# FFT and mixture of experts on one core: batch 2 transformed ahead of the first expert slot, scale products tied

## The chip, the cores and the metric

One core of a Trainium2 chip. The metric is the device time of one execution in microseconds (us); less is better. The engines are TensorE (PE; its weight loads are PEld), VectorE (DVE), ScalarE (ACT), GpSimd (POOL) and SyncE (SP), which here only issues DMAs.

## The reference

```python
X = np.fft.fft(x, axis=1)          # x: 8 x 2496 x 256
x = np.fft.fft(X, axis=2).real.reshape(19968, 256)
logits = x @ w_gate                # 8 experts
e_idx = np.argmax(logits, axis=1)
...
for e in range(8):
    mask = e_idx == e
    h = np.maximum(x[mask] @ w1[e], 0.0)     # 256 -> 1024
    ye = h @ w2[e]                           # 1024 -> 256
    out[mask] = gate_w[mask, None] * eom[mask, e, None] * ye
```

Each batch of 2496 rows goes through a two-dimensional Fourier transform, of which the real part is kept; each row then goes to the one expert that its gate picks, and the result is scaled by two gate values.

## The kernel before, in words

**Transform.** A batch comes as five column chunks (`xt`, 512 KB each). Each chunk is folded: `fold1` adds its halves (line 419), `fold2` makes sums and differences (`ft`, lines 437 to 452), and its squares are summed for a scale. `dstage` multiplies a chunk with a table (fp32 matmuls, line 492) into PSUM (`psb_t`, three buffers), and `devac` splits the result into two fp16 parts, `ahi` by ScalarE and `alo` by VectorE (lines 504, 505). `sstage(b, i)`, for i from 0 to 4, does the second transform in fp16 (line 556), and `sevac` makes rows of it (`eo`, `rt`, `rows`; lines 575 to 594). `gatepass` (line 537) computes the gates of batches 0 and 1 first; for the others the gate columns ride in `sstage`. `gating` finds expert, position and scale of each row (`desti`, `car`).

**Scatter.** `send` writes the rows into a scratch tensor `scr` in DRAM, sorted by expert: 20 indirect DMAs of 128 rows per batch, on GpSimd (line 705). Four DMAs of SP write zero rows at the end of the same tensor (line 1055).

**Experts.** Work is cut into slots of up to 256 rows. Round 0 has 16 slots (8 experts x 512 rows) and takes rows of batches 0 and 1 only, rounds 1 and 2 take rows of the batches up to 3 and up to 5, and a last part the rest. A slot loads its rows as `xr` (a transposing DMA) and their scale words `xf` (lines 1198, 1199); SP issues both. `mm1` computes `hp` (line 1266), `hh` and `hl` are its two fp16 parts (lines 1270, 1271), and `mm2` computes `yp` (line 1288). `ysc` is the product of the row's scale and the expert's (line 1292, VectorE, 128x2 elements), `y` the scaled result (line 1295), and GpSimd scatters it to the output. Weights of an expert are loaded in fp32 (`load_w`, line 1208), squared for a scale (`wenergy`, 1221; `wscale`), and split into two fp16 parts (`conv`, lines 1242 and 1243).

**Order.** `start` is written out by hand for all engines. In the second part, up to the first slots, only SP and GpSimd follow the written order (`PH1`); the order on TensorE, VectorE and ScalarE is set at build time by a scheduler, which works with its own estimates of when a DMA lands. VectorE's and ScalarE's queues are in order: an instruction that waits holds up all behind it. `steps` yields a step for each `sstage`: steps 0 to 9 are batches 0 and 1, 10 to 14 batch 2. `WEND` is the step after which the first slots' code is begun, `FSTART` the one after which slots and further steps alternate; PSUM is divided anew there (`hp` gets two buffers, `yp` one). `behind(eng)` has an instruction placed after the newest `hh` or `hl` of the slots, and `pin` keeps folds in the written order.

```python
MARGIN0 = 1
FSTART = 5 * BA + MARGIN0     # BA = 2
WEND = FSTART - 2
```

## Time and profile before

| | |
|---|---|
| median of 3 runs | 1108.4 us (1107.82 to 1110.0) |
| the profiled execution | 1108.73 us |
| its span, first to last instruction | 1107.0 us |
| TensorE busy | 1042.2 us (94%) |
| VectorE busy | 672.9 us (61%) |
| ScalarE busy | 598.9 us (54%) |
| GpSimd busy | 428.2 us (39%) |
| mean granted clock of TensorE | 0.979 |
| first slot's first matmul | 125.34 us |

All times in rows are from the start of the span. "Idle before" names what released an engine after it stood still. A busy share is a mean over stages with different limits, so it is to be read by stage. The granted clock is a share of full speed.

### The profile page before, as it was taken

How to read it: one execution, taken by the hardware profiler on the slowest of the kernel's cores; microseconds unless marked ns; L12 is line 12 of the kernel's file. 1: busy time of each engine (PE TensorE's matmuls, PEld its weight loads, DVE VectorE, ACT ScalarE, POOL GpSimd, SP SyncE). 2: the span in 40 equal slices, each digit the busy share in tenths (PEclk: the TensorE clock that was granted, in tenths of full speed). 3: DMA queues.
4: the chain of work that ended last, by engine and by line, in shares of the span. 5: the costliest groups of instructions: out<-in, count | busy, mean ns of one | idle time of the engine just before them, and what ended most of it. 6: DMA issues, size and time to landing. Idle time of an engine off the chain costs nothing. (4 is left out here: it accounts for less than half of the span.)

```text
span 1107.0 us, 27910 instructions
## 1 busy us (share of the span) xinstructions
PE 1042.2 (94%) x10226; PEld 934.3 (84%) x10226; DVE 672.9 (61%) x1351; ACT 598.9 (54%) x1099; POOL 428.2 (39%) x389
## 2 busy tenths in 40 slices
PE   5795598999998999999999999999999999999998
PEld 4584587888887999999998888888998979998997
DVE  5875558869689468557559554554355553555542
ACT  3366376667677456556554554544445553555542
POOL 0267114566478363436255771221221222212122
PEclk9897799999999999999999999999999999999999
DMA  9525373665577436556465896646556565575640
GB/s 367 182 77 189 118 186 102 166 188 183 132 175 201 101 111 156 132 154 168 130 174 121 205 198 165 158 96 180 137 134 189 143 173 130 149 165 159 156 102 28
DMA packets 152312, 171.02 MB, mean 154 GB/s; under 512 B 115309, under 2 KB 116207, under 8 KB 152164
## 3 DMA queue, kind: packets, MB, share of 16 engines
q1 hardware_dynamic: 136292, 126.48, 44.5%
q0 software_dynamic: 15728, 42.14, 11.7%
q8 instruction: 82, 1.34, 0.5%
q10 hardware_dynamic: 144, 0.52, 0.2%
q14 instruction: 66, 0.54, 0.2%
HBM read 149.51 MB, written 43.63 MB: 174 GB/s over the span
## 5 line engine op out<-in xcount | busy, mean ns | idle before, releaser
L1266 PE MATMUL hp<-xr,w0b 128*128 128x256 f16 (+2 forms) x4080 | 477.2, 267 | 11.3 <-DVE hl L1271 11.2
L1288 PE MATMUL yp<-w1b,hh 128*128 128x256 f16 x2560 | 438.5, 273 | 0.8 <-ACT y L1295 0.8
L1266 PEld LDWEIGHTS <-w0b 128*128 128x128 f16 x4080 | 380.8, 98 | 56.6 <-issue 10.4
L1296 POOL DMA_INDIRECT out_dram<-y,xf x160 | 188.7, 1179 | 549.7 <-ACT y L1295 501.0
L1288 PE MATMUL yp<-w1b,hl 128*128 128x256 f16 x1280 | 349.2, 273 | 0.0
L1271 DVE SCALAR_TENSOR_TENSOR hl<-hp,hh 128x512 f16<-128x512 f32 (+2 forms) x340 | 221.0, 654 | 204.0 <-ACT hh L1270 179.4
L1270 ACT ACTIVATE hh<-hp 128x512 f16<-128x512 f32 (+2 forms) x340 | 191.8, 567 | 247.0 <-PE hp L1266 244.7
L1288 PEld LDWEIGHTS <-hh 128*128 128x128 f16 x2560 | 248.1, 98 | 28.6 <-issue 1.3
L705 POOL DMA_INDIRECT scr<-rows,desti x160 | 173.0, 1081 | 59.2 <-issue 42.4
L1288 PEld LDWEIGHTS <-hl 128*128 128x128 f16 x1280 | 125.8, 98 | 14.6
L1295 ACT ACTIVATE y<-yp,ysc 128x256 f32<-128x256 f32 (+1 forms) x160 | 67.5, 470 | 43.7 <-PE yp L1288 39.2
L1243 DVE SCALAR_TENSOR_TENSOR w0b<-raw0b,wsc,w0b 128x1024 f16<-128x1024 f32 x44 | 58.3, 1325 | 48.5 <-ACT w0b L1242 48.5
L1243 DVE SCALAR_TENSOR_TENSOR w1b<-raw1b,wsc,w1b 128x1024 f16<-128x1024 f32 x44 | 56.4, 1283 | 39.6 <-ACT w1b L1242 37.9
L492 PE MATMUL psb_t<-tdet,ft 128*125 128x290 f32 (+1 forms) x200 | 60.7, 457 | 14.0 <-DVE alo L505 4.7
L1242 ACT ACTIVATE w0b<-raw0b,wsc 128x1024 f16<-128x1024 f32 x44 | 50.3, 1146 | 32.9 <-PE hp L1266 31.5
L492 PEld LDWEIGHTS psb_t<-tdet,ft 128*125 128x125 f32 (+1 forms) x200 | 40.5, 212 | 28.9 <-issue 12.9
L1242 ACT ACTIVATE w1b<-raw1b,wsc 128x1024 f16<-128x1024 f32 x44 | 50.4, 1147 | 14.4 <-PE yp L1288 13.2
L419 POOL TENSOR_TENSOR xt<-xt 128x500 f32<-128x500 f32 (+1 forms) x25 | 32.5, 1308 | 63.1 <-DMA xt<-in_xl_dram 28.8
L1243 DVE SCALAR_TENSOR_TENSOR w1b<-raw1b,ssc,w1b 128x1024 f16<-128x1024 f32 x32 | 41.0, 1282 | 23.7 <-ACT w1b L1242 22.8
L1243 DVE SCALAR_TENSOR_TENSOR w0b<-raw0b,ssc,w0b 128x1024 f16<-128x1024 f32 x32 | 40.8, 1282 | 22.0 <-ACT w0b L1242 21.5
L1242 ACT ACTIVATE w0b<-raw0b,ssc 128x1024 f16<-128x1024 f32 x32 | 36.4, 1145 | 14.3 <-DMA raw0b<-in_w_dram 13.2
L505 DVE SCALAR_TENSOR_TENSOR alo<-psb_t,p_x,ahi 125x580 f16<-125x580 f32 (+1 forms) x40 | 32.0, 816 | 19.1 <-ACT ahi L504 19.0
(221 smaller groups left out, 1008.4 us busy)
## 6 DMA issues: line engine op xcount, KB each, us to landing
raw0b<-in_w_dram SPq DMA_DIRECT2D x118, 512.0 KB
raw1b<-in_w_dram SPq DMA_DIRECT2D x118, 512.0 KB
xt<-in_xl_dram SPq DMA_DIRECT2D x40, 512.0 KB
scr<-rows,desti POOLq DMA_INDIRECT x160
out_dram<-y,xf POOLq DMA_INDIRECT x160
xr<-scr SPq DMA_TRANSPOSE x85
xf<-scr SPq DMA_DIRECT2D x75, 2.0 KB
tst<-in_ts_dram SPq DMA_DIRECT2D x2, 512.0 KB
```

The lines of the kernel that those rows point to most:

```text
L419: i = eng.tensor_tensor(x0, x0, x1, op=ALU.add)
L492: nc.tensor.matmul(o[:, 0:290], ft[:, k, par, W], tdab[:, k], start=(k == 0), stop=(k == 1))
L505: nc.vector.scalar_tensor_tensor(s["alo"][W, c], ps[W, :, 0:290], sc, s["ahi"][W, c], op0=ALU.mult, op1=ALU.subtract)
L705: free_order("scr", batch=b, inst=nc.gpsimd.indirect_dma_start(out=scr[:, :], out_offset=bass.IndirectOffsetOnAxis(ap=s["desti"][:, j:j + ...
L1242: nc.scalar.activation(w[:, 0], r, AF.Copy, scale=sc)
L1243: nc.vector.scalar_tensor_tensor(w[:, 1], r, sc, w[:, 0], op0=ALU.mult, op1=ALU.subtract)
L1266: nc.tensor.matmul(ps[:, k, T], w1v[:, hl, kc, (f % 4) * 128:(f % 4 + 1) * 128], a["x"][:, x, T], start=(m == 0), stop=(m == 5))
L1270: i = nc.scalar.activation(hh[:, G, T], ps[:, :, T], AF.Relu)
L1271: j = nc.vector.scalar_tensor_tensor(hl[:, G, T], ps[:, :, T], 0.0, hh[:, G, T], op0=ALU.max, op1=ALU.subtract)
L1288: nc.tensor.matmul(a["yp"][0:M, u], a[k, h][:, f, u * 128:u * 128 + M], w2v[:, hl, f], start=(g == 0 and f == 0 and m == 0), stop=(h == 1 ...
L1295: nc.scalar.activation(a["y"][0:M, u], a["yp"][0:M, u], AF.Copy, scale=ys[0:M, u:u + 1])
L1296: put = nc.gpsimd.indirect_dma_start(out=out[:, :], out_offset=bass.IndirectOffsetOnAxis(ap=a["f"].bitcast(I32)[0:M, u, 1:2], axis=0), in_ ...
```

## The change

Its parts:

- `FSTART` goes from 11 to 14 and `WEND` from 9 to 10, so all of batch 2's five steps are emitted before slots and steps alternate. Loads of the first slots and of the next weights, and `load_x`, now come at step 10; the second expert's four weight loads follow the first two `xr` and `xf` together.
- The four DMAs of zero rows move from behind the first weight loads into `start`, behind the loads of the tables.
- Batch 2's five `fold1` go from GpSimd to VectorE, and its folds are handed out in pieces behind the first gating and in steps 0 to 2 (`foldall`, `some`). Batch 3's folds may start at step 5 as before, but now all through `folds`.
- The second `gatepass` comes at step 2 instead of 1. The first expert's weights are squared at steps 1 and 2 instead of 6, scaled at step 4 instead of 8, and converted at steps 8 and 9 (w1) and 10 (w2).
- `ysc` is placed behind the newest `hl` (`behind("DVE")`) in rounds 0 to 2; before the last part the notes of the newest instructions are cleared.

```diff
--- before.py
+++ after.py
@@ -61,10 +61,10 @@
 SPL = (4, 9, 14)
 MARGIN = 2 + len(SPL)
 
-MARGIN0 = 1
+MARGIN0 = 4
 FSTART = 5 * BA + MARGIN0
 
-WEND = FSTART - 2
+WEND = 5 * BA
 
 AHEAD = (5, 6, 7, 8, 9)
 
@@ -376,7 +376,7 @@
         gens = []
         hold = []
 
-        newest, pinned = {}, []
+        newest, pinned, final = {}, [], []
 
         def behind(eng):
             return tc.issue_after(newest[eng]) if eng in newest else nullcontext()
@@ -983,6 +983,8 @@
                 load_t(j)
             fold(4)
             nc.sync.dma_start(tidt, tid)
+            for k in range(4):
+                nc.sync.dma_start(scr[DUM + 128 * k:DUM + 128 * (k + 1), :], ztile)
             scale(0)
             smalls.clear()
             for c in range(KC):
@@ -1002,7 +1004,7 @@
                 m = fq[0]
                 fq[0] += 1
                 dve = m // KC <= BA + 1
-                if m < NB * KC and m // KC != BA:
+                if m < NB * KC:
                     fold1(*divmod(m, KC), nc.vector if dve else nc.gpsimd)
                 while fq[1] < NB * KC and fq[1] <= m - (0 if fq[1] // KC <= BA + 1 else FLAG):
                     f = fold2(*divmod(fq[1], KC))
@@ -1023,6 +1025,18 @@
                 else:
                     p = None
 
+        def foldall(b):
+            for c in range(KC):
+                fold1(b, c, nc.vector)
+                yield
+                for _ in fold2(b, c):
+                    yield
+                yield
+
+        def some(g, k):
+            for _ in range(k):
+                next(g, None)
+
         def dparts(b):
             for c in range(KC):
                 dstage(b, c)
@@ -1040,8 +1054,6 @@
             folds(0, 2 * KC - 1)
             xcap[0] = NB * KC
             load_x()
-            for c in range(KC):
-                fold1(BA, c, nc.gpsimd)
             gatepass(0)
             add_gen(gating(0))
             for _ in sstage(0, 0):
@@ -1051,11 +1063,11 @@
             for m in range(2):
                 for h in range(2):
                     load_w(0, m, h)
-            for k in range(4):
-                nc.sync.dma_start(scr[DUM + 128 * k:DUM + 128 * (k + 1), :], ztile)
             weave(piece("A"))
+            fa = foldall(BA)
             weave(piece("C"), dparts(1))
             weave(piece("C"))
+            some(fa, 12)
             for n in range(5 * BA):
                 b, i = divmod(n, 5)
                 if n:
@@ -1064,22 +1076,23 @@
                     for _ in sevac(b, i):
                         pass
                 send(b, i)
-                if n == 1:
+                some(fa, 3 if n < 2 else 99)
+                if n == 2:
+                    fq[:] = 2 * [KC * (BA + 1)]
                     gatepass(1)
                     add_gen(gating(1))
-                ahead((0, 0, 12, 12, 99)[min(n, 4)])
+                ahead((0, 0, 8, 12, 99)[min(n, 4)])
                 if n == 4:
                     for _ in table_a(0):
                         pass
-                if n >= 5:
-                    folds(n, KC * BA + i, [])
-                if n == 6:
-                    for m in range(2):
-                        for h in range(2):
-                            wenergy(0, m, h)
-                if n == 8:
+                if n in (1, 2):
+                    for h in range(2):
+                        wenergy(0, n - 1, h)
+                if n == 4:
                     for m in range(2):
                         wscale(sched[0][1], m)
+                if n > 7:
+                    conv(0, 0, n - 8)
                 yield ("step", n)
             for n in range(5 * BA, 5 * NB):
                 b, i = divmod(n, 5)
@@ -1106,6 +1119,9 @@
                 next(sv)
                 for _ in sv:
                     pass
+                if n == 5 * BA:
+                    for h in range(2):
+                        conv(0, 1, h)
                 if i == 1 + (b == BA) and b + 1 < NB:
                     energy(b + 1)
                     energy_sum(b + 1)
@@ -1242,7 +1258,7 @@
                 nc.scalar.activation(w[:, 0], r, AF.Copy, scale=sc)
                 nc.vector.scalar_tensor_tensor(w[:, 1], r, sc, w[:, 0], op0=ALU.mult, op1=ALU.subtract)
             nxt = (after_new if wb == 0 else after_sing).get(n, NS)
-            if n or m:
+            if n:
                 chained(load_w, nxt, m, h)
             else:
                 late.append((nxt, m, h))
@@ -1269,7 +1285,7 @@
             hh, hl = a["hh", g // 2], a["hl", g // 2]
             i = nc.scalar.activation(hh[:, G, T], ps[:, :, T], AF.Relu)
             j = nc.vector.scalar_tensor_tensor(hl[:, G, T], ps[:, :, T], 0.0, hh[:, G, T], op0=ALU.max, op1=ALU.subtract)
-            if sched[n][0] < LAST:
+            if sched[n][0] < LAST and not final:
                 newest.update(ACT=getattr(i, "ins", i), DVE=getattr(j, "ins", j))
 
         def mm2(n, g):
@@ -1289,7 +1305,8 @@
                                      start=(g == 0 and f == 0 and m == 0), stop=(h == 1 and f == 3 and m == 2), skip_group_check=U == 2)
             ys = a["ys"]
             if g == 2:
-                nc.vector.tensor_scalar(ys[:, 0:U], a["f"][:, 0:U, 0], scale_of(n, 2), None, op0=ALU.mult)
+                with behind("DVE"):
+                    nc.vector.tensor_scalar(ys[:, 0:U], a["f"][:, 0:U, 0], scale_of(n, 2), None, op0=ALU.mult)
             if g == 3:
                 for u in range(U):
                     nc.scalar.activation(a["y"][0:M, u], a["yp"][0:M, u], AF.Copy, scale=ys[0:M, u:u + 1])
@@ -1347,8 +1364,6 @@
         late = []
 
         def experts():
-            for h in range(2):
-                conv(0, 0, h)
             yield "w"
             chained(load_x_, 0)
             hold.clear()
@@ -1384,9 +1399,7 @@
                                 wenergy(nb, *what)
 
                     p = n - 1 + g % 2
-                    if p < 0:
-                        conv(0, 1, g // 2)
-                    elif p in next_new:
+                    if p in next_new:
                         conv(next_new[p], (g + 1) % 2, g // 2)
                     if todo:
                         k, m, h = todo[0]
@@ -1465,6 +1478,8 @@
                 fx.append(pl(ctx, name="fr", bufs=2, side="right"))
                 fg = experts()
                 next(fg)
+                next(fg)
+                load_x()
             if m == ("step", FSTART):
                 break
         pps.close()
@@ -1473,8 +1488,6 @@
         psf.update(hb=2, yb=1)
         pool["b"] = pl(pps, name="psb2", bufs=2, space=PS)
         pool["m"] = pl(pps, name="psm2", bufs=1, space=PS)
-        next(fg)
-        load_x()
         bg = background()
 
         ends = [n - 2 for n in range(1, NS) if sched[n][0] != sched[n - 1][0]]
@@ -1489,6 +1502,8 @@
                 acc -= next(bg, 1.0)
             if LAST in ready:
                 break
+    final.append(1)
+    newest.clear()
     with tc.manual_schedule():
         for m in fg:
             pass
```

What this moves, on VectorE: before, around the last first-transform results of batch 2 (`alo`) and the first slot's `ysc`:

```order
L477 TENSOR_SCALAR lsc<-lsc 128x1
L505 SCALAR_TENSOR_TENSOR alo<-psb_t,p_x,ahi 125x580 x4
L1292 TENSOR_SCALAR ysc<-xf,wsc 128x2
L505 SCALAR_TENSOR_TENSOR alo<-psb_t,p_x,ahi 128x580
L419 TENSOR_TENSOR xt<-xt 128x4x125 x2
L1292 TENSOR_SCALAR ysc<-xf,wsc 128x2
L437 TENSOR_TENSOR ft<-xt 128x2x125 x2
```

and now the place of the first `ysc`, in the second slot:

```order
L661 TENSOR_REDUCE r_dest<-r_t 128x20
L664 TENSOR_TENSOR desti<-r_dest,cs 128x20
L276 TENSOR_SCALAR p_w<-psm_t 128x1
L277 TENSOR_SCALAR wsc<-p_w 128x1
L278 TENSOR_SCALAR wiv<-p_w 128x1
L1287 SCALAR_TENSOR_TENSOR hl<-hp,hh 128x512
L1309 TENSOR_SCALAR ysc<-xf,wsc 128x2
L1259 SCALAR_TENSOR_TENSOR w0b_138<-raw0b_134,wsc,w0b_138 128x1024
```

The first `ysc` stood between two `alo` of batch 2, ahead of any `hl`; it now stands behind six `hl`, and no `ysc` stands ahead of them.

On VectorE, where the indices `desti` of batch 0 are made, before:

```order
L661 TENSOR_REDUCE r_dest<-r_t 128x20
L682 SCALAR_TENSOR_TENSOR car<-r_se,p_x,r_num 128x20
L505 SCALAR_TENSOR_TENSOR alo<-psb_t,p_x,ahi 125x580 x2
L664 TENSOR_TENSOR desti<-r_dest,cs 128x20
L505 SCALAR_TENSOR_TENSOR alo<-psb_t,p_x,ahi 125x580
L505 SCALAR_TENSOR_TENSOR alo<-psb_t,p_x,ahi 128x580
L582 SCALAR_TENSOR_TENSOR eo<-psb_t,qb 128x258 x2
```

and now:

```order
L661 TENSOR_REDUCE r_dest<-r_t 128x20
L682 SCALAR_TENSOR_TENSOR car<-r_se,p_x,r_num 128x20
L419 TENSOR_TENSOR xt<-xt 128x4x125
L505 SCALAR_TENSOR_TENSOR alo<-psb_t,p_x,ahi 125x580 x2
L664 TENSOR_TENSOR desti<-r_dest,cs 128x20
L437 TENSOR_TENSOR ft<-xt 128x2x125
L441 TENSOR_TENSOR xt<-xt 128x2x125
L419 TENSOR_TENSOR xt<-xt 128x4x125
L505 SCALAR_TENSOR_TENSOR alo<-psb_t,p_x,ahi 125x580
```

One fold of batch 2 stands ahead of the indices, the others between batch 1's `alo` and the row groups of batch 0. On GpSimd's queue the difference at the start is:

```order
 L256 MEMSET ztile 128x258
 L257 MEMSET ztile 128x1
+L705 DMA scr<-rows,desti 161280x258 x40
 L419 ISA
 L419 TENSOR_TENSOR xt<-xt 128x4x125 x4
 L419 TENSOR_TENSOR xt<-xt 128x512
-L705 DMA scr<-rows,desti 161280x258 x40
```

The 40 scatters of batches 0 and 1 now come first, and the folds behind them are those of batch 4.

On TensorE the second transform of batch 2 had 48 of its 180 matmuls (line 556) ahead of the first `hp`; now it has all 180 there, and the 20 fp32 products of batch 3's first transform (line 492) stand between them.

## Rows read from the trace of the kernel before

**Rows 1.** Busy time by stretch (length, PE, PEld, DVE, ACT, POOL, PEclk, DMA, GB/s):

```profile
0.00:30.00 30.00, 17.36 (x99) 13.47 (x100) 18.15 (x51) 11.44 (x22) 0.63 (x7) 1.00 0.95 364
30.00:80.00 50.00, 43.31 (x727) 39.01 (x724) 40.27 (x117) 23.48 (x57) 23.10 (x20) 0.90 0.37 123
80.00:125.34 45.34, 21.29 (x110) 16.78 (x106) 23.80 (x61) 22.16 (x46) 27.28 (x26) 0.70 0.50 166
125.34:360.00 234.66, 222.19 (x2128) 198.17 (x2126) 185.54 (x404) 161.58 (x331) 126.79 (x114) 0.99 0.60 163
360.00:1107.00 747.00, 738.01 (x7181) 666.82 (x7178) 405.09 (x721) 380.21 (x644) 250.36 (x225) 1.00 0.56 145
```

**Rows 2.** TensorE's waits in the whole span: us in total, times, longest:

```profile
PE psb_t L556 <- DVE alo L505: 13.3, 1, 13.3
PE hp L1266 <- DVE hl L1271: 11.2, 9, 2.4
...
PE yp L1288 <- ACT y L1295: 0.8, 1, 0.8
```

**Rows 3.** Timeline at the first slot (start, us, instruction, idle before):

```profile
120.10 0.23 DVE L1292 TENSOR_SCALAR ysc<-xf,wsc 128x2 f32<-128x2 f32 x1 [13.74 <-DMA xf<-scr]
...
121.10 0.28 PE L556 MATMUL psb_t<-alo,tst 128*128 128x145 f16 x1 [13.30 <-DVE alo L505]
```

**Rows 4.** Timeline of zero rows, indices and scatters (SP, DVE, POOL):

```profile
44.05 2.03 SPq L1055 DMA_DIRECT2D scr<-ztile  x4
50.61 0.17 DVE L664 TENSOR_TENSOR desti<-r_dest,cs 128x20 int32<-128x20 f32 x1
55.23 1.12 POOL L705 DMA_INDIRECT scr<-rows,desti  x1 [8.44 <-DVE alo L505]
...
70.19 1.26 POOL L705 DMA_INDIRECT scr<-rows,desti  x1 [3.72 <-ACT rows L702]
...
113.93 0.97 POOL L705 DMA_INDIRECT scr<-rows,desti  x1 [0.30 <-issue]
```

**Rows 5.** Busy time by stretch, for the last two columns, DMA:

```profile
20.00:30.00 10.00, 8.57 (x73) 6.36 (x72) 8.08 (x19) 3.93 (x7) 0.01 (x1) 1.00 0.98 397
...
50.00:52.00 2.00, 2.00 (x6) 1.39 (x5) 0.78 (x2) 0.00 (x0) 0.00 (x0) 0.50 1.01 384
...
54.00:56.00 2.00, 2.00 (x22) 1.62 (x22) 0.74 (x1) 0.74 (x1) 0.77 (x1) 1.00 0.00 0
```

**Rows 6.** Timeline of a fold on GpSimd and VectorE beside and after it:

```profile
29.99 2.63 POOL L419 TENSOR_TENSOR xt<-xt 128x500 f32<-128x500 f32 x2 [28.76 <-DMA xt<-in_xl_dram]
30.04 1.47 DVE L441 TENSOR_TENSOR xt<-xt 128x250 f32<-128x250 f32 x1
...
33.59 0.42 DVE L441 TENSOR_TENSOR xt<-xt 128x250 f32<-128x250 f32 x1
```

**Rows 7.** VectorE's busy time from 50 to 110, and single prices from the timeline:

```profile
50.00:110.00 60.00, 46.18 (x592) 39.69 (x591) 39.95 (x111) 36.58 (x80) 39.96 (x36) 0.86 0.39 137
...
120.97 1.26 DVE L419 TENSOR_TENSOR xt<-xt 128x500 f32<-128x500 f32 x2
123.17 0.74 DVE L437 TENSOR_TENSOR ft<-xt 128x250 f32<-128x250 f32 x2
105.54 0.82 DVE L505 SCALAR_TENSOR_TENSOR alo<-psb_t,p_x,ahi 125x580 f16<-125x580 f32 x1 [3.32 <-ACT ahi L504]
125.91 0.76 DVE L587 TENSOR_TENSOR rt<-eo 128x258 f32<-128x258 f32 x2
126.77 0.83 DVE L582 SCALAR_TENSOR_TENSOR eo<-psb_t,qb 128x290 f32<-128x290 f32 x2
127.91 0.70 DVE L590 TENSOR_TENSOR rows<-rt,rows 128x516 f16<-128x516 f32 x1 [0.31 <-ACT rows L589]
...
83.43 1.04 ACT L1221 ACTIVATE wsq<-raw0b 128x1024 bf16<-128x1024 f32 x1
```

**Rows 8.** Timeline of TensorE: 30 second-transform matmuls, then `hp`; one first-transform chunk, then `yp`:

```profile
127.65 0.24 PE L556 MATMUL psb_t<-ahi,tstm 125*128 125x145 f16 x1 [0.84 <-DVE eo L582]
...
129.57 1.47 PE L1266 MATMUL hp<-xr,w0b 128*128 128x256 f16 x12
...
146.56 2.13 PE L492 MATMUL psb_t<-tdet,ft 128*125 128x290 f32 x8
148.52 0.27 PE L1288 MATMUL yp<-w1b,hl 128*128 128x256 f16 x1
```

## The prediction

> **What bounds the kernel now.** I first cut the span into stages (busy time by stretch). From 125 us on TensorE is the limit: it works 738.01 of the last 747.00 us and 222.19 of the 234.66 us before them [rows 1]. Before 125.34 us, where the first expert product starts, it is not: 12.6 us idle up to 30 us, 6.7 us up to 80 us, and 24.0 us of the 45.34 us after that, at a granted clock of 0.70, a mix of its two levels of 1.2 and 2.4 GHz [rows 1]. So the question is what holds TensorE between 80 and 125 us, and whether the change lets work in there.
>
> Next I read TensorE's list of waits: one wait stands out, 13.3 us, once, for `alo` from VectorE [rows 2]. The timeline shows its cause. At 120.10 VectorE runs `ysc`, a product of 128x2 elements of the first slot, after 13.74 us in which it waited for the DMA of `xf`; the last `alo` of batch 2 is the next in its queue, and TensorE resumes at 121.10 [rows 3]. `xf` is read from the scratch rows after all 40 scatters of batches 0 and 1, and the last of these starts at 113.93 [rows 4]. So one small instruction, issued too early in VectorE's order, makes VectorE, and through it ScalarE and TensorE, wait for GpSimd's scatters.
>
> Those scatters begin late: the first starts at 55.23, though its indices were there at 50.78 (50.61 + 0.17) [rows 4]. The zero rows went to the same scratch tensor at 44.05, behind four weight loads; the DMA engines are full at 50 to 52 us and silent at 54 to 56 [rows 4, 5]. I read this as the scatters waiting for that write to land.
>
> **The change part by part.** *Scale products tied.* `ysc` of slot 0 now stands behind the second slot's second `hl`. Its `xf` has long landed there, since the same slot's matmuls need the `xr` loaded just before it. The stop of 13.74 us on VectorE goes; what is late next is the work itself, below.
>
> *First slot's text later.* With 14 instead of 11 as the last step before the slots, TensorE does, ahead of the first `hp`, everything it did before plus the rest of batch 2's second transform, 60+36+36 = 132 matmuls, and batch 3's first transform, 5 chunks. Thirty such matmuls take 129.57 - 127.65 = 1.92 us, so 132 take 8.4 us; a chunk takes 148.52 - 146.56 = 1.96 us, five take 9.8 us [rows 8]. That is 18.2 us of work moved ahead of the first slot. If the first `hp` starts at T1 and nothing later changes, the span is T1 + (1107.00 - 125.34) - 18.2 = T1 + 963.5 us. The change breaks even at T1 = 143.5. So T1 is what must be worked out, from three sides.
>
> *T1 from the rows in the scratch (GpSimd).* Zero rows: four DMAs move on SP's queue ahead of batch 2's five loads and the weights. There the engines are full (0.98, 397 GB/s [rows 5]), so their 0.53 MB push batch 2's loads back by 1.3 us; VectorE wants those only at about 45 us, and one had landed at 29.99 before [rows 6], so this costs nothing. Without it the five loads would lie on VectorE's path. The scatters may then start when the indices are there. These come sooner too: the five folds on GpSimd stretch VectorE's instructions beside them, as 1.47 against 0.42 us for the same line [rows 6]; I count five such, 4.7 us in all. One fold of batch 2 (0.63 us [rows 7]) is put ahead of the indices. So the first scatter starts at about 47 instead of 55. This is not all kept: the second group of four needs rows that pass VectorE and ScalarE, where batch 2's folds and squares now stand in front; I put it at 59. From 70.19 to 114.90 a scatter took 1.40 us (32 of them [rows 4]); 36 take 50.4, and I add 3 us because the four weight squares (1.04 us each, plus a readout [rows 7]) now delay the rows of the next groups on ScalarE: 112 against 114.90. From there to the landed `xf` it took 5.2 us (114.90 to 120.10): x at 117.
>
> *T1 from VectorE.* It was busy 39.95 us from 50 to 110 [rows 7]. To this come: five folds of batch 2 and five of batch 3, 0.63 to 0.67 each, 6.6; batch 3's second fold, 10 instructions at 0.37 to 0.42 for the chunks, four more for two pairs and two short ones, 6.4; its five `alo` at 0.82, 4.1; batch 2's five row groups, 0.83 + 0.76 + 0.70 each and one without the first, 10.6; the start of its gating, about 2 (single prices in [rows 7]). That is 29.7 us more, 69.6 in all. It starts from 50.8 - 4.7 = 46, so it ends at 115.6 if VectorE never waits. It waited 20 of those 60 us before, mostly for TensorE's chunks, and the folds fill most of that. I keep two waits: 2 us where the gate's copy stands behind the squares on ScalarE, and 4 to 6 where batch 2's chunks free PSUM one by one. The first `hl` is thus at 122 to 124, its `hp` 2 us before.
>
> *T1 from TensorE.* It was busy 17.36 + 43.31 + 21.29 = 82.0 us up to the first `hp` [rows 1], plus 18.2 is 100.2. The 12.6 us of the start stay: 113. Its waits in 30 to 107 us (6.7 and some 10 outside the 13.3) shrink but don't vanish; I take half of these 17.4: 121.7.
>
> The three give 117, 120 to 122 and 122. I take **T1 = 122**, the top, since waits of VectorE and TensorE on each other add up. Span 122 + 963.5 = 1085.5. The profiled execution took 1108.73 for a span of 1107.0, so 1.7 lie around it: **1087.2 us**. (The median of the runs is 0.3 us below that execution.) The ends: without VectorE's waits T1 is 115; with 16 of its old 20 us, and not the 6 to 8 I keep, it is 130.
>
> *The rest.* The squares, scales and weight conversions are the same instructions at earlier places, and VectorE's share of them is in the 39.95. The second expert's w2 loads now follow directly on the first slots' x loads on SP; they are needed two slots later. Batch 3's loads follow the earlier folds into the stretch 30 to 80 us, where the DMA engines are 0.37 busy [rows 1]. GpSimd loses five folds. Later idle time (12.5 us up to 360, [rows 1]) may move by 4 us either way: 16 slots now carry 11 steps instead of 14, which helps the 11.2 us that `hp` waits for `hl` [rows 2], but the order of everything is new.
>
> **The rivals.** *More goes than the stop* (chance 0.09). VectorE's waits vanish, T1 = 115, and a third of the later 12.5 us goes: 115 + 963.5 + 1.7 - 4 = 1076. For it: fewer steps beside the first slots. Against: PSUM still hands batch 2's chunks on one by one.
>
> *The scatters become the bound* (0.07). VectorE has little idle time left beside them. The 1.40 us are a mean over a stretch in which it was idle for the last third. If a scatter took 1.8 us beside a VectorE that never rests, x comes at 59 + 36 x 1.8 + 3 + 5.2 = 132; TensorE, at its first `hp` with batch 3 queued behind it, waits: T1 = 133, 1098 us. By the Trainium skill ("SBUF — State Buffer", Who interferes with whom) two-input additions on VectorE block GpSimd's reads but not its writing of descriptors, which only copies, casts and scalar products in a two-port mode hold up; by it the folds moved here would not stretch the scatters and x would come at 117. The rows agree for the reads (1.47 against 0.42); none isolates the descriptors.
>
> *Nothing is gained* (0.03). The order is only reshuffled: what is taken out before T1 comes back as waits of the first round, whose rows of batches 2 and 3 must be scattered before slot 16. Then 1107. Against: the last of their scatters stands in GpSimd's queue behind the outputs of eleven slots, as before.
>
> *Slower* (0.03). `ysc` now waits for the newest `hl`. There is one `yp` buffer in these slots, so if VectorE is behind, `y` is late and the next slot's `yp` waits. This decides where it costs over 21.5/48 = 0.45 us in each of the 48 slots that are tied; at 0.7 us it gives 1087.2 + 33.6 = 1121 us. Against: TensorE waited for `y` once, 0.8 us [rows 2], and it waits for `hl` only nine times, so VectorE is seldom behind.
>
> **How the numbers follow.** The forecast has 0.78. T1 from 115 to 130 and 4 us of later idle time either way give 1076 to 1099; 1077 to 1099 leaves out half of the first rival, the last two, and a little of each side, under 0.2. What a measurement of this kernel can tell from no change is about 0.2%, 2.2 us. Faster by more: 0.78 + 0.09 + 0.07 = 0.94; within: 0.03; slower: 0.03.
>
> **What would show it.** Right: no wait of VectorE on `xf` near the first slot; the first scatter before 50 us and the last near 111; the first `hp` near 122 with `psb_t` matmuls up to it; VectorE over 80% busy from 50 to 120; the granted clock near 1.0 after 95 us. Wrong: a first `hp` after 130, TensorE waiting for `xr`, waits of `yp` for `y` in every slot, or more than 17 us idle between 125 and 360.

## The result, and the profile after

The changed kernel takes 1092.39 us (median of 4 runs, 1090.91 to 1093.92) against 1108.11 us for the kernel before on the same chip: a ratio of 0.985, 95% interval 0.9828 to 0.9872. It is 15.7 us faster; the forecast was 20.9 faster. The profiled execution took 1091.5 us for a span of 1089.6.

The stages of the changed kernel, busy time by stretch (length, PE, PEld, DVE, ACT, POOL, PEclk, DMA, GB/s), cut where TensorE stops and where its first `hp` starts; they answer to [rows 1]:

```profile
0.00:30.00 30.00, 17.81 (x117) 13.93 (x118) 18.59 (x52) 11.44 (x22) 0.62 (x6) 1.00 0.96 353
30.00:80.00 50.00, 43.88 (x726) 40.53 (x722) 44.38 (x144) 33.24 (x77) 19.27 (x17) 0.90 0.53 187
80.00:122.90 42.90, 35.91 (x262) 28.59 (x262) 33.31 (x77) 27.46 (x61) 26.61 (x23) 0.88 0.31 97
122.90:137.58 14.68, 0.00 (x1) 0.01 (x1) 7.06 (x9) 0.44 (x2) 6.51 (x5) 0.66 0.72 288
137.58:360.00 222.42, 218.83 (x2128) 197.72 (x2128) 164.19 (x368) 154.00 (x309) 121.16 (x110) 0.99 0.59 163
360.00:1089.60 729.60, 719.41 (x7003) 650.32 (x7001) 395.19 (x709) 373.21 (x630) 245.66 (x224) 1.00 0.57 146
```

From 80 us on TensorE now works 35.91 of 42.90 us, where it had worked 21.29 of 45.34 [rows 1]. At 122.9 all that stands ahead of the first slot is done. Then it does nothing for 14.68 us. TensorE's waits, to be set against [rows 2]:

```profile
PE hp L1282 <- DVE eo L582: 14.7, 1, 14.7
...
PE hp L1282 <- DVE hl L1287: 5.7, 5, 2.0
```

The 13.3 us wait for `alo` is gone, and one for `eo`, 1.4 us longer, stands in its place. The timeline shows where it comes from (start, us, instruction, idle before; DVE, POOL, PE and SP together):

```profile
34.86 0.17 PE L537 MATMUL psm_t<-alo,tstq 128*128 128x16 f16 x1 [2.05 <-issue]
...
49.24 0.16 DVE L664 TENSOR_TENSOR desti<-r_dest,cs 128x20 int32<-128x20 f32 x1
50.33 1.44 POOL L705 DMA_INDIRECT scr<-rows,desti  x1 [49.10 <-DVE xt L441]
...
59.78 1.49 POOL L705 DMA_INDIRECT scr<-rows,desti  x1 [3.97 <-ACT rows L702]
...
72.68 1.30 POOL L705 DMA_INDIRECT scr<-rows,desti  x1 [1.93 <-ACT rows L702]
...
112.40 0.97 POOL L705 DMA_INDIRECT scr<-rows,desti  x1 [0.30 <-issue]
115.05 1.35 SPq L1214 DMA_TRANSPOSE xr<-scr  x1
117.83 1.24 SPq L1214 DMA_TRANSPOSE xr<-scr  x1
121.42 0.82 DVE L505 SCALAR_TENSOR_TENSOR alo<-psb_t,p_x,ahi 128x580 f16<-128x580 f32 x1 [0.54 <-ACT ahi L504]
122.14 17.80 SPq L310 DMA_DIRECT2D xt<-in_xl_dram  x7
129.25 6.60 POOL L419 TENSOR_TENSOR xt<-xt 128x500 f32<-128x500 f32 x5 [15.87 <-issue]
130.52 4.21 DVE L437 TENSOR_TENSOR ft<-xt 128x250 f32<-128x250 f32 x3 [8.28 <-POOL xt L419]
134.65 2.13 DVE L441 TENSOR_TENSOR xt<-xt 128x250 f32<-128x250 f32 x3
136.71 0.81 DVE L582 SCALAR_TENSOR_TENSOR eo<-psb_t,qb 128x290 f32<-128x290 f32 x2
137.58 2.74 PE L1282 MATMUL hp<-xr,w0b 128*128 128x256 f16 x12 [14.68 <-DVE eo L582]
```

To be read from the bottom. The first `hp` waits for the last reader of batch 2's PSUM, `eo`. Ahead of that `eo`, VectorE's queue holds three pairs of second folds of batch 4 (lines 437 and 441). They wait 8.28 us for GpSimd's first folds. GpSimd stood still for 15.87 us before these; its row names no releaser, but they read batch 4's x loads, and those SP issues only at 122.14, because the row loads `xr` stand ahead of them in its queue and wait for the last scatter (112.40). So far this is a reading of the timeline; experiments 1 and 2 test it. It is the pattern of [rows 3] again: an instruction that nobody needs yet holds up a queue in order.

### The profile page after: what moved, and what is told of

Its sections match the earlier page's. It is cut to its first block, busy times and chain, and to the rows that moved or that the text cites. A ratio compares the mean times of both kernels' runs of the same rounds, so it can differ in the third digit from the quotient of the medians.

```text
span 1089.6 us, 27921 instructions
## 1 busy us (share of the span) xinstructions
PE 1035.8 (95%) x10226; PEld 931.1 (85%) x10226; DVE 662.7 (61%) x1356; ACT 599.8 (55%) x1099; POOL 419.8 (39%) x384
## 5 line engine op out<-in xcount | busy, mean ns | idle before, releaser
L1282 PE MATMUL hp<-xr,w0b 128*128 128x256 f16 (+2 forms) x4080 | 476.8, 266 | 20.5 <-DVE eo L582 14.7
L1313 POOL DMA_INDIRECT out_dram<-y,xf x160 | 186.3, 1165 | 537.0 <-ACT y L1312 491.9
L1259 DVE SCALAR_TENSOR_TENSOR w0b<-raw0b,wsc,w0b 128x1024 f16<-128x1024 f32 x44 | 61.8, 1404 | 61.7 <-ACT w0b L1258 61.7
L492 PE MATMUL psb_t<-tdet,ft 128*125 128x290 f32 (+1 forms) x200 | 59.0, 448 | 13.1 <-DVE rt L575 5.3
L1258 ACT ACTIVATE w1b<-raw1b,ssc 128x1024 f16<-128x1024 f32 x32 | 36.7, 1145 | 9.8 <-DMA raw1b<-in_w_dram 9.0
```

What stands on the lines that cost most here:

```text
L492: nc.tensor.matmul(o[:, 0:290], ft[:, k, par, W], tdab[:, k], start=(k == 0), stop=(k == 1))
L1258: nc.scalar.activation(w[:, 0], r, AF.Copy, scale=sc)
L1259: nc.vector.scalar_tensor_tensor(w[:, 1], r, sc, w[:, 0], op0=ALU.mult, op1=ALU.subtract)
L1282: nc.tensor.matmul(ps[:, k, T], w1v[:, hl, kc, (f % 4) * 128:(f % 4 + 1) * 128], a["x"][:, x, T], start=(m == 0), stop=(m == 5))
L1313: put = nc.gpsimd.indirect_dma_start(out=out[:, :], out_offset=bass.IndirectOffsetOnAxis(ap=a["f"].bitcast(I32)[0:M, u, 1:2], axis=0), in_ ...
```

## The experiments

The theory (A): the 14.7 us come from batch 4's folds, which stand in VectorE's queue ahead of `eo` and wait for loads that stand behind `xr` in SP's queue. The rivals have their letters in the expectations. Medians, with the ratio to the kernel before in runs on the same chip; T1 is the start of the first `hp`, "rest" the span less T1, both of the profiled run:

| kernel | us | ratio (95%) | T1 | rest |
|---|---|---|---|---|
| before, profiled run | 1108.7 | | 125.34 | 981.7 |
| the change | 1092.4 | 0.985 (0.9828 to 0.9872) | 137.58 | 952.0 |
| 1 loads first | 1080.8 | 0.9761 (0.9733 to 0.979) | 126.37 | 952.5 |
| 2 folds later | 1078.8 | 0.9745 (0.9709 to 0.9781) | 123.07 | 955.1 |
| 3 tie undone | 1093.0 | 0.9867 (0.9837 to 0.9898) | 139.62 | 952.7 |
| 4 before with the tie | 1100.7 | 0.9943 (0.9924 to 0.9962) | 120.25 | 979.6 |
| 5 zero rows late | 1089.3 | 0.9848 (0.9825 to 0.9871) | 135.24 | 951.8 |
| 6 folds on GpSimd | 1098.2 | 0.9921 (0.9891 to 0.9951) | 140.83 | 956.8 |
| 7 MARGIN0 = 1 | 1097.3 | 0.9916 (0.9895 to 0.9938) | 117.51 | 979.0 |
| 8 both edits, 1 and 2 | 1078.8 | 0.9751 (0.9726 to 0.9775) | 123.87 | 952.0 |

### 1. Batch 4's loads ahead of the first rows

```diff
                 next(fg)
-                next(fg)
+                hold.clear()
                 load_x()
+            if m == ("step", FSTART - 1):
+                next(fg)
```

> Edit: the changed kernel, with batch 4's five x loads issued by SP ahead of the first slots' row loads (xr, xf) and not behind them; the order on VectorE is the same to the instruction. Theory A (the 14.7 us in which the first hp waited come from batch 4's folds, which stand in VectorE's queue ahead of eo and wait for loads that stood behind xr on SP): the loads are issued near 100 to 105 us, GpSimd folds from 113 to 120, the first hp comes at 124 to 128, the time is 1079 to 1083 us. Theory B (the rows of the first slot, or the handover of PSUM, would have held the first hp nearly as long): the first hp stays at 133 or later, now waiting for xr or for a PSUM reader, and the time is 1088 to 1093 us.

The timeline of this kernel:

```profile
104.35 2.82 SPq L310 DMA_DIRECT2D xt<-in_xl_dram  x5
114.74 6.08 POOL L419 TENSOR_TENSOR xt<-xt 128x500 f32<-128x500 f32 x5
117.90 1.35 SPq L1214 DMA_TRANSPOSE xr<-scr  x1
123.52 1.07 DVE L437 TENSOR_TENSOR ft<-xt 128x250 f32<-128x250 f32 x3
126.37 1.49 PE L1282 MATMUL hp<-xr,w0b 128*128 128x256 f16 x12 [2.44 <-DVE eo L582]
```

Nothing on VectorE was moved, only five DMAs on SP, and TensorE's wait falls from 14.68 to 2.44 us. The folds in front of `eo` now cost their own work, some 2 us from 123.52 on. Theory A; B falls.

### 2. Batch 4's folds behind the first slot

```diff
-KC * (BA + 1) + (1, 4, 5, 6, 9, 99)[min(n - 5 * BA, 5)]
+KC * (BA + 1) + (1, 4, 4, 4, 4, 9, 99)[min(n - 5 * BA, 6)]
```

> Edit: the changed kernel, with all folds of batch 4 held back to the step after the first slot is begun, so that eo of batch 2's last step follows the last alo in VectorE's queue; the loads stay where they are. Theory A: no wait of VectorE on GpSimd's folds near 122 us, the first hp at 123 to 126 us; the folds come later beside the first slots, and the time is 1077 to 1083 us. Theory B: the first hp at 133 or later all the same, 1088 to 1093 us.

```profile
120.73 2.39 SPq L310 DMA_DIRECT2D xt<-in_xl_dram  x5
122.19 0.82 DVE L582 SCALAR_TENSOR_TENSOR eo<-psb_t,qb 128x290 f32<-128x290 f32 x2 [1.15 <-ACT qb L580]
123.07 1.48 PE L1282 MATMUL hp<-xr,w0b 128*128 128x256 f16 x12 [1.36 <-DVE eo L582]
```

The same wait, taken away from its other end: the loads come nearly as late as before (120.73 against 122.14), but nothing ahead of `eo` needs them. The rows of the first slot were there, so they were not the bound. The first twelve `hp` take 1.48 us instead of 2.74: TensorE had stood still for 1.36 us and not for 14.68, and starts at a granted clock of 1.00 (2.4 GHz), where it was 0.50 (1.2 GHz) over these matmuls in the changed kernel.

### 3. The change without the tie of the scale products

The edit takes `with behind("DVE")` from `ysc`.

> Edit: the changed kernel with the scale products ysc not tied to the newest hl. Two ysc now stand in VectorE's queue between batch 2's row groups, near 107 us. Theory A: VectorE stops there until xf has landed near 120 us, some 12 us, but the 10 us of work behind it is done by about 131, when batch 4's folds come from GpSimd anyway; the two waits overlap, the first hp comes at 138 to 141 us and the time is 1090 to 1095 us. Theory C (the tie is what the change gains, and the waits add up): the first hp near 150, 1102 us or more.

```profile
118.89 0.23 DVE L1308 TENSOR_SCALAR ysc<-xf,wsc 128x2 f32<-128x2 f32 x1 [12.45 <-DMA xf<-scr]
119.90 0.59 PE L470 MATMUL psm_t<-es,cs 128*128 128x1 f32 x2 [11.72 <-DVE es L466]
...
139.62 2.74 PE L1282 MATMUL hp<-xr,w0b 128*128 128x256 f16 x12 [3.01 <-DVE eo L582]
```

The old stop returns, 12.45 us, and yet the first `hp` comes only 2.0 us later: the two waits lie over each other. The stop puts the last `alo` off from 121.42 to 135.70, and behind it VectorE no longer waits for the folds, which GpSimd makes meanwhile (129.97 to 136.91). In this kernel the tie is worth next to nothing; what it is worth where the loads are not late (number 8) no run shows.

### 4. The kernel before with the tie alone

```diff
             if g == 2:
-                nc.vector.tensor_scalar(ys[:, 0:U], ...)
+                with behind("DVE"):
+                    nc.vector.tensor_scalar(ys[:, 0:U], ...)
```

The notes of the newest instructions are cleared ahead of the last part, as in the change.

> Edit: the kernel before, with the scale products tied to the newest hl and nothing else. Theory A: the 13.3 us wait of TensorE for alo goes, but the rows of the first slot still come no sooner than about 120 us, since the scatters start as late as before; only the 4.2 us of TensorE's work between the wait and the first hp move into the gap, and the first hp comes at 120 to 122: 1102 to 1106 us. Theory C (the tie is what the change gains): 1092 to 1096 us.

```profile
120.25 2.74 PE L1266 MATMUL hp<-xr,w0b 128*128 128x256 f16 x12 [8.63 <-DMA xr<-scr]
```

A ratio of 0.9943, some 6 us. The 13.3 us wait of [rows 2] became one of 8.6 for the rows themselves: the stop on VectorE had covered TensorE's lack of other work. The mechanism of A is right; the time is 1.3 us below its range. I had left the rest as it was, though the 4.2 us of work moved ahead of T1 had to come off it; it fell by 2.1, and the kernel before was itself 1.4 us faster on this chip (1106.7 against 1108.1).

### 5. Zero rows back behind the weights

The edit moves the four `dma_start(scr[...], ztile)` back behind the first `load_w`.

> Edit: the changed kernel with the four DMAs of zero rows back behind the first weight loads; the order on VectorE and GpSimd is the same. The step of the prediction: the scatters wait for the zero rows, so the first starts near 55 us and not at 50. Theory R (the scatters are then held by the rows, for which GpSimd stands still 4.0 and 1.9 us in the changed kernel, at 59.8 and 72.7): these pauses take up the 5 us, the last scatter starts at 112.4 to 113.5 and the time is 1091 to 1094 us, no difference that can be measured. Theory Z (the start of the scatters carries through to the end): last scatter at 116 to 118, the first hp and the time later by 4 to 5 us, 1096 to 1098 us. The first scatter at 50 as before would say that the zero rows never held it.

Indices and scatters of this kernel:

```profile
46.78 0.18 DVE L664 TENSOR_TENSOR desti<-r_dest,cs 128x20 int32<-128x20 f32 x1
51.07 1.15 POOL L705 DMA_INDIRECT scr<-rows,desti  x1 [49.84 <-DVE ft L450]
...
57.32 1.49 POOL L705 DMA_INDIRECT scr<-rows,desti  x1 [0.79 <-ACT rows L702]
...
109.94 0.97 POOL L705 DMA_INDIRECT scr<-rows,desti  x1 [0.30 <-issue]
```

The indices were there at 46.96, the first scatter came 4.1 us later; with early zero rows it came 0.9 us behind them. So the scatters did wait for the zero rows, as I read in [rows 4]. (The row names `ft` on VectorE as the releaser; in numbers 9 and 11, with late zero rows too, the gap is 4.6 and 4.5 us and the row names another engine.) But the pause at the second group shrank from 3.97 to 0.79 us and took most of it, as theory R has it. Last scatter (109.94) and time (1089.3) are even below R's ranges, which began at 112.4 and 1091. What no theory had: the indices were 2.4 us sooner (46.96 against 49.40). With early zero rows TensorE waited 2.05 us at 34.86 in the gate's product with the table `tstq`, which is loaded just ahead of them; here that wait is missing. Over the change and numbers 1 to 3 and 6 to 8, all with early zero rows, it is 0 to 2.3 us; in the kernel before and in number 5 it is 0. The profile names no releaser; that the zero rows slow the table's DMA is my reading, and not the whole of it: number 7 has no such wait, and its indices still come at 48.45. The time is that of the change (0.9848 against 0.985): this part gains nothing that can be measured.

### 6. Batch 2's first folds on GpSimd

In `foldall`, `fold1(b, c, nc.gpsimd)` instead of `nc.vector`.

> Edit: the changed kernel with batch 2's five first folds on GpSimd, at the same place of the text: four now stand ahead of the first scatter in GpSimd's queue and one behind the eighth. Theory R: five folds of 1.25 to 1.5 us are 6 to 7.5 us of GpSimd, of which 2 to 4 go into its pauses; VectorE's folds beside them take up to three times as long. The last scatter comes at 115 to 118, and the time is 1094 to 1099 us. Theory N (the engine of these folds doesn't matter, as all of it goes into pauses): 1090 to 1093 us.

```profile
32.35 2.77 POOL L419 TENSOR_TENSOR xt<-xt 128x500 f32<-128x500 f32 x2 [31.13 <-DVE ft L437]
35.65 2.85 POOL L419 TENSOR_TENSOR xt<-xt 128x500 f32<-128x500 f32 x2 [0.52 <-DMA xt<-in_xl_dram]
...
63.35 1.21 POOL L705 DMA_INDIRECT scr<-rows,desti  x1 [7.30 <-ACT rows L702]
68.38 1.30 POOL L419 TENSOR_TENSOR xt<-xt 128x512 f32<-128x512 f32 x1
...
115.69 0.97 POOL L705 DMA_INDIRECT scr<-rows,desti  x1 [0.31 <-issue]
```

The last scatter is 3.3 us later and the time worse than the change's, by 6 us in the medians (1098.2 against 1092.4) and 8 in the ratios (0.9921 and 0.985). Theory R. Moving these folds to VectorE is a real part of the gain.

### 7. The slots as early in the text as before

`MARGIN0 = 1`, all else as in the change.

> Edit: the changed kernel with MARGIN0 = 1 as before, so that slots and steps alternate from step 11 on; all other parts of the change stay. Theory A (batch 2's transform is what fills the time until the rows are there): the first hp waits for xr at 118 to 121 us, TensorE stands still 10 us or more ahead of it, the 15 to 18 us of transform come later, and the time is 1095 to 1101 us, 3 to 9 more than with the change although the 14.7 us wait for eo is gone. Theory D (the place of the text is worth nothing by itself): 1078 to 1085 us, since the wait for eo goes.

```profile
117.51 2.72 PE L1282 MATMUL hp<-xr,w0b 128*128 128x256 f16 x12 [11.48 <-DMA xr<-scr]
```

TensorE stands 11.48 us ahead of its first `hp`, now for the rows. The wait for `eo` is gone, the first `hp` is 20 us sooner than in the change (0.5 us sooner than A had it), and still the kernel is 5 us slower in the medians, 7 in the ratios. So filling the time until the rows come is the core of the change, and D falls.

### 8. Loads first and folds later

Both edits of 1 and 2 together.

> Edit: both edits together, batch 4's loads issued ahead of the first xr and its folds held back to the step after the first slot is begun. Theory A (each edit alone takes away the whole wait of the first hp for the folds): nothing more to gain but TensorE's waits for hl in the first slots, 1076 to 1080 us. Theory F (each removes only a part of it): 1070 to 1075 us.

```profile
123.87 1.48 PE L1282 MATMUL hp<-xr,w0b 128*128 128x256 f16 x12 [1.36 <-DVE eo L582]
```

Each edit had taken away the same wait, so nothing adds up; theory A. This kernel and number 2 are the best of the study, 28 us faster than the kernel before where the change gives 15.7.

Busy time by stretch, number 7 and then number 8, up to their first `hp` and after it (in 360 to 700 us TensorE is busy throughout in both):

```profile
0.00:117.51 117.51, 78.98 (x934) 67.54 (x935) 88.08 (x253) 64.46 (x144) 46.91 (x46) 0.88 0.56 198
117.51:360.00 242.49, 233.25 (x2228) 208.60 (x2228) 178.29 (x388) 158.28 (x319) 127.93 (x116) 0.98 0.60 167
...
700.00:1096.50 396.50, 386.53 (x3783) 348.79 (x3781) 194.71 (x282) 195.22 (x314) 83.03 (x76) 0.99 0.55 139
```

```profile
0.00:123.87 123.87, 96.71 (x1098) 82.60 (x1099) 98.61 (x274) 72.67 (x161) 52.59 (x51) 0.93 0.61 214
123.87:360.00 236.13, 231.10 (x2266) 209.23 (x2267) 172.89 (x385) 158.78 (x320) 129.50 (x119) 1.00 0.58 165
...
700.00:1075.90 375.90, 365.73 (x3593) 329.93 (x3590) 184.22 (x268) 184.66 (x298) 78.14 (x72) 1.00 0.53 138
```

### 9 to 12. Two further parts, on chips that could not tell

Number 9 is number 8 with late zero rows; number 10 is the change with the weight squares back at step 6 and their scale at step 8. They ran on another chip, and as 11 and 12 once more on a third.

> Edit: loads first and folds later, as in the run with both edits, and the four DMAs of zero rows back behind the first weight loads. Theory R (the early zero rows gain nothing, as the scatters' pauses take up their delay, and cost 0 to 2.3 us of TensorE at 31 to 35 us, where the gate's matmuls with tstq wait when the zero rows go beside that table on the DMA engines): the first scatter waits again for the zero rows, 4 us behind its indices, and starts near 51; no wait of TensorE at tstq; the first hp at 121.5 to 123.5, the time 1073 to 1077.5 us, 1 to 4 less than with both edits alone. Theory N (where the zero rows stand is worth nothing either way): 1077.5 to 1080 us. Theory Z (a later first scatter carries through): the first hp at 126 or later, waiting for xr, 1081 us or more.

> Edit: the changed kernel with the first expert's four weight squares and their scale back at steps 6 and 8. The step of the prediction: the squares (four of 1.04 us, each with a readout) stand on ScalarE ahead of the rows of the next groups and delay the scatters by 3 us. Theory S (they do): GpSimd's pause near 72 us shrinks, the last scatter starts 1.5 to 3 us sooner, near 109.5 to 111, and with it xr, the loads behind it and the first hp: 1089 to 1091 us. Theory N (the squares go into ScalarE's pauses): the last scatter at 112 to 113, 1091 to 1094 us. Theory L (late squares hold up the weight conversions): the first hp waits for w0b, 1094 us or more.

> The same kernel as in the run with both edits and late zero rows, on another chip: there the kernel before took 1158 us and TensorE stood still again and again for up to 1.1 us with no releaser, so nothing of it could be set beside the other runs. If the kernel before is near 1107 us here: theory R: first scatter near 51, 4 us behind its indices, no wait of TensorE at tstq, first hp at 121.5 to 123.5, ratio to before 0.970 to 0.974. Theory N: ratio 0.974 to 0.977. Theory Z: first hp at 126 or later, ratio over 0.977.

> The same kernel as in the run with late squares, on another chip, for the same reason. If the kernel before is near 1107 us here: theory S (the early squares delay the scatters): last scatter at 109.5 to 111, ratio 0.982 to 0.984. Theory N: last scatter at 112 to 113, ratio 0.984 to 0.987. Theory L (late squares hold up the weight conversions, or the order around them): the first hp at 139 or later, ratio over 0.987.

On these two chips the kernel before took 1157.6 and 1166.8 us, where the chips of the other runs gave 1106.7 to 1108.1. Number 9 came to 1138.3 (ratio 0.9862, 0.9814 to 0.991), 11 to 1150.0 (0.986, 0.9828 to 0.9891), 10 to 1141.5 (0.9878, 0.9822 to 0.9934), 12 to 1147.0 (0.9843, 0.9809 to 0.9877). The times of the expectations were set for a kernel before near 1107 us, so none of them can be held against these. TensorE's waits in number 11 tell why this cannot be set beside the rest:

```profile
PE psb_t L556 <- issue: 13.7, 21, 1.2
PE yp L1304 <- issue: 11.9, 15, 1.5
PE hp L1282 <- issue: 6.4, 9, 2.3
```

These are stops with no releaser, 32 us in all; in the list of number 8 no such row of these products stands. They are not the whole difference: the profiled span is 1148.4 us, number 8's 1075.9. With them the first `hp` comes at 150.6 us. Two things could still be read. In 9 and 11 no wait stands at `tstq`, and in 11 the first scatter starts at 50.83, 4.5 us behind its indices (46.36): the zero rows held it, as in number 5. The squares give no answer: with late ones, in 12, the last scatter starts at 122.74, against 120.84 in 11 with early ones, but in 10 with late ones at 118.26, against 120.07 in 9. The two pairs point opposite ways, and their kernels differ in more. Whether late zero rows improve number 8, and what the early squares cost, stays open.

## Why the prediction was right, and where it was wrong

**The total.** The direction and the size were right: 1092.4 us against 1087.2 and a range of 1077 to 1099. But two terms of the sum missed by more than the total shows: T1 was 137.58 and not 122, 15.6 late, and the rest was 952.0 and not 963.5, 11.5 short. The span missed by the difference, 4.1. That the total came so near is luck in this: the two misses have opposite signs, and nothing in the prediction ties one to the other.

**What bounds the kernel, and the old stop.** Right. The wait of `ysc` for `xf` is gone, and experiments 3 and 4 bring it back and take it away by the tie alone.

**T1 from TensorE.** Right for the end of its work, 122.9, where 121.7 was worked out. Its two terms missed against each other: 97.6 us busy up to there and not 100.2, and 13.1 us of waits after 30 us, not 8.7.

**T1 from GpSimd.** Right where it counted: second group at 59.78 (forecast 59), the last scatter done at 113.37 (112). The low end T1 = 115, in the range and in the first rival, overlooked this side: its own sum has the rows there at 117. The first one missed, 50.33 against 47. The step that failed is the zero rows: "this costs nothing" left out that the indices come up to 2.4 us later (experiment 5), and their gain went into the pause that I had allowed for.

**T1 from VectorE.** This step failed. Its work was right: 59.1 us busy in 50 to 120, 84% where over 80% was named, and the last `alo` at 121.42. But the list that I priced ends with batch 3 and the start of batch 2's gating. Batch 4's folds stand in the same piece of the queue, ahead of `eo`; I took the queue's end for granted and did not ask of every instruction ahead of the first slot whose data it needs and when they are issued. The text says "the second expert's w2 loads now follow directly on the first slots' x loads on SP", and does not say that batch 4's loads come behind these. By experiments 1 and 2 this one omission cost 12 to 14 us in the medians, 10 to 12 in the ratios.

**The moved work.** This term was mis-sized. 18.2 us were moved ahead of T1, priced at full speed. Against the kernel before, the rest holds 22.0 us less busy time (960.20 against 938.24, the last two stretches of each table), so of the 11.5 us that it came out short 3.8 are busy time, whose source no run shows, and 7.7 idle time. Numbers 4 and 7, without the move, have a rest of 979 to 980 us; the change and numbers 1, 3, 5 and 8, with it, one of 952 to 953, and numbers 2 and 6 one of 955 and 957. Number 7 differs from the change in `MARGIN0` alone, so there the move is worth 27 us of the rest.

Where the 27 us come from, numbers 7 and 8 show. The stretches after T1 give number 8 22.95 us less busy time than number 7 (959.78 against 936.83, the 340.00 between them included in both) and 4.0 us less idle time. Ahead of T1 number 8 is busy 17.7 us longer (96.71 against 78.98), near my 18.2. Of the 5.2 us beyond that, the clock gives most, by an estimate: in stretches of 3 us number 7's granted clock is 0.50 and 0.59 from 117.51 to 123.51, and 0.65 and 0.78 from 183.51 to 189.51, behind another stop of 2.23 us; busy time times the missing share is 4.4 us, where number 8 loses none up to 360. TensorE resumes after its wait at half clock (0.50, 1.2 GHz), twelve `hp` in 2.72 us where 1.48 is full speed. The changed kernel, which stops too, has no such gain over the kernel before: by the same estimate it loses 1.9 us from T1 to 360, and that one 1.7.

**Later idle time.** I allowed 4 us either way. It fell by 7.7: from 12.5 and 9.0 us [rows 1] to 3.6 and 10.2. The waits of `hp` for `hl` fell from 11.2 [rows 2] to 5.7; with MARGIN0 = 1 they are 9.8. That fewer steps beside the first slots help them was right; that it was 7.7 us and not up to 4 is the larger part of the 11.5.

**The rivals.** The scatters did not become the bound. From 59.78 to 112.40 there are 35 steps and one pause of 1.93 us, 1.45 us each, with VectorE 89% busy beside them up to 80 us and 86% after that; 1.8 was the price of the rival. By the Trainium skill ("SBUF — State Buffer", Who interferes with whom) two-input additions of VectorE do not hold up GpSimd's descriptors; the trace agrees, as the 1.45 us are near the 1.40 of the kernel before, where VectorE was 64% busy in that stretch. The rival with a price for the tie did not come: no wait of `yp` for `y` is left in the list. What did come, a new wait in the place of the old, is near the rival with 0.03, but not by its mechanism: that one had the first round wait for scattered rows, and this wait is for batch 4's loads, at the first slot. The shorter rest hid it.

**What would show it.** Held: no wait on `xf`, the last scatter near 111, VectorE over 80% busy. Not quite: the first scatter before 50 (50.33), a granted clock near 1.0 after 95 us, which was 0.94 up to 122.9, and `psb_t` matmuls up to the first `hp`. Of the signs against it "a first `hp` after 130" came true: it was right about the step, although the time lies in the range. The idle time from 125 to 360 us, 16.2, was just under the 17 named.

## What to carry to other kernels

When work is moved ahead of a point, list everything that stands in front of that point in each engine's queue, work of later batches too, and for each entry find when its DMA is issued and what stands ahead of that DMA in its queue. Two waits in one place hide each other: undoing one part of a change (3) can show nothing where the same part alone (4) shows 6 us. And work that fills a wait of TensorE can take more than its own time off the rest, here 27 us for 18: between numbers 7 and 8 some 4 us of the difference are clock, by the estimate above, and 4 are idle time.

## What the runs showed of the hardware

The same kernel differed by 4.6% to 5.4% between chips: before took 1107 us on some and 1158 and 1167 us on two others, with 32 us of stops without a releaser on TensorE in number 11, each at most 2.3 us. Each chip was used at one time only, so what makes the difference is open. Times are compared here by the ratio to runs on one chip.

VectorE's second folds beside GpSimd's first folds took 4.21 us for three (line 437, at 130.52), while three take 1.07 us at 123.52 in experiment 1, where GpSimd had finished: a factor of 3.9. One alone is 1.45 us long there and 0.41 in experiment 1, a factor of 3.5, as in [rows 6]. They follow each other at 1.40 us, about as long as one of GpSimd's folds (6.60 us for five, 1.32 each). By the Trainium skill ("SBUF — State Buffer", Who interferes with whom) a VectorE instruction with two inputs in SBUF contends with a GpSimd instruction that reads SBUF, and the port pair that the two share is an exclusive lock. The trace agrees, as VectorE's instructions are longer beside GpSimd's. That the two take turns is my reading: each second fold also needs the result of one of these first folds, which alone would space their starts.
